# Sums of a linear-attention and GELU kernel in other TensorE tiles, and one more block of seven products

## The chip, the cores and the metric

The kernel runs on one core of a Trainium2 chip. Its time is the device time of the whole program in microseconds (us). The kernel before took 260.33 us as the median of three runs (260.18 to 260.61).

## The reference

First comes an attention without softmax. Queries and keys of 4 batches, 4 heads, 1088 tokens and 32 channels are each sketched twice (8 values each), and the outer product of the two sketches gives 64 features. Then

```
kv  = einsum('bhsf,bhsd->bhfd', k_p, v)
z   = sum(k_p, axis=2)
num = einsum('bhsf,bhfd->bhsd', q_p, kv)
den = einsum('bhsf,bhf->bhs', q_p, z)[..., None] + 1e-06
x   = (num / den), heads side by side: 4352 tokens x 128
out = gelu_exact(x @ w_in) @ w_out        # 128 -> 2048 -> 128
```

Everything is computed in float32. The two weight matrices arrive as 64-bit floats and are rounded to 32 bits on the chip.

## The kernel before, in words

The tokens are cut into eight chunks of 512, two for each batch (numbers 0 to 7), and one last chunk (8) with the 64 left-over tokens of each batch. The hidden width of 2048 is 16 pieces of 128, numbered by fi. The main loop (L1094) walks over a list `steps` of (chunk, fi); one entry is one step t. A step computes one hidden piece on TensorE (`hidden`, L686), ScalarE takes its GELU (L699), and a few steps later TensorE projects it back with `w_out`.

There are two ways to project. The plain way (`project`, L816) is one 128x128 matmul over 512 tokens for each fi. The other takes four pieces fi together as a block and does the two-by-two block multiplication with seven products instead of eight (`two_products`, L763). GpSimd forms the sums of tokens (`token_sums`, L733: four instructions, written to `bits_low`, `bits_a`, `bits_e`, `bits_m`) and once for each weight piece the sums of channels (`channel_sums`, L718: four instructions). TensorE then does seven pairs of 128x64 products over 256 tokens. The pairs are called fours, ones, sixes and twos after their names in the code; fours read `bits_low`, ones `bits_a`, sixes `bits_e`, twos `bits_m`. `drain` (L781) and `combine` (L806) put a chunk's results together. `USUAL = 8` says that chunks 0 and 1 take the first eight fi plainly. Their plain steps alternate, four by four: chunk 0 fi 0 to 3, chunk 1 fi 0 to 3, chunk 0 fi 4 to 7, chunk 1 fi 4 to 7; then chunk 0 fi 8 to 15, chunk 1 fi 8 to 15, and chunk 2 onward.

Among the steps stand pieces of the attention of later batches. They are entered by hand under a step number with `at(t, ...)` (L935), and within an engine the instructions stay in the order of the text (L1148 to L1154). For batches 1 to 3:

- `key_turn_blocks` (L356) and `features_of_all` (L939) sketch the keys: eight 64x32 matmuls. `outer_of_all` (L949) and `add_tokens` (L965) make the features and their sums over a partition's tokens, `k_s`, on VectorE. `turn_keys_rem` and `features_rem` (L985, L989) do the same for the left-over tokens with two 128x128 matmuls.
- `finish_keys` (L992) computes kv with `kv_sum` (L431): 36 matmuls of 128x32 tiles, 64 columns each, and z with `z_sum` (L440): four more. ScalarE copies kv out and `turn_kv` (L455) transposes it. `fold_z` (L446) writes z into the query sketch `S_abc`.
- `query_sketch` (L557) and `attend` (L605) are eight 64x32 matmuls each; `query_outer` (L574) between them is VectorE's. `turn_first_kv` (L499) does for batch 0, in four 128x32 matmuls, what `z_sum` does for the others.

PSUM has two banks for hidden pieces, two for projections, and two double banks (`work_banks`, L67) for the attention. `round_at` (L999) rounds a weight piece of 512 columns in two steps, with ScalarE and VectorE, for two pieces with a last product on GpSimd.

Of the kernel before, what the change touches and what calls it, by code (L numbers as in the profile page):

```python
# [8 lines left out]
FP = mybir.dt.float32  # L9
# [7 lines left out]
def kernel(  # L17
# [21 lines left out]
    F = R * R  # L39
# [13 lines left out]
    NMAIN = B * NCH  # L53
    NB = 4

    USUAL = 8
    NCHUNK = NMAIN + 1
    assert B == 4 and d_model == 128 == H * D == JC * D == 2 * F and H == 4 and REM == 64 and NCH == 2

# [7 lines left out]
    def work_banks():  # L67

        return wps.tile([128, 2, CW], FP, name="w_ps")
# [159 lines left out]

    kz_first = big.tile([128, 128], FP, name="kz_first")  # L230

    ones = big.tile([128, D], FP, name="ones")

    v_rem_aug = [big.tile([128, H, D if b else 2 * D], FP, name=f"v_rem_aug{b}") for b in range(B)]
    pool.memset(v_rem_aug[0], 0.0)
    pool.memset(v_rem_aug[0][:REM], 1.0)
    dve.memset(ones, 1.0)

    v_aug = [att.tile([128, NP, J, 2 * D], FP, name="sums") for r in range(2)]
    for t in v_aug:  # L240
# [185 lines left out]
    def kv_product(ps, lhsT, features, h, part, start=False, stop=False):  # L426

        pe.matmul(ps[h * D:(h + 1) * D, part * F:(part + 1) * F], lhsT=lhsT, rhs=features, start=start, stop=stop,  # L428
                  skip_group_check=True)
# [9 lines left out]

    def z_sum(b):  # L440

        ps = held["kv"][:, 0]
        for h in range(H):
            kv_product(ps, ones, k_s[b][:, h], h, 1, start=True, stop=True)

    def fold_z(b):  # L446
        sketch_of_z(b, held["kv"][:, 0], F)

    kv_T = {}

# [48 lines left out]
    def turn_first_kv():  # L499

        ps, zs = work_bank(), held["zs"]
        for h in range(H):
            c, r = h // 2, h % 2
            pe.matmul(ps[h * D:(h + 1) * D, :F], lhsT=zs[:, r], rhs=ident[:, c * F:(c + 1) * F], start=True, stop=True)
        sketch_of_z(0, ps, 0)


# [178 lines left out]
    def hidden(n, fi, by_halves=False):  # L686
        W = width[n]
        ps = first_banks.pop((n, fi)) if (n, fi) in first_banks else hidden_bank()
        w = w_tile(w_in_sb, fi)
        for rows in (slice(0, 64), slice(64, 128)) if by_halves else (slice(0, 128),):  # L690
            if (n, fi) not in begun:
                pe.matmul(ps[rows, :W], lhsT=w[:, rows], rhs=xT[n][:, :W], start=True, stop=True)  # L692
        if n < NCH and fi < USUAL:
# [5 lines left out]
        act.activation(out=g_of[n, fi][:, :W], in_=ps[:, :W], func=ACT.Gelu)  # L699
# [58 lines left out]
        return sums[n, b][j][:, e], T[j][:, k]  # L758

    def first_block(n):  # L760
        return USUAL // NB if n < NCH else 0

    def two_products(n, b, i):  # L763

        fours, ones_, sixes = [("4", "7", e, e) for e in range(2)], [("1", "5", e, e) for e in range(2)], ("6a", "6b", 0, 1)

        opens = b == first_block(n)
        order = fours + ([sixes] + ones_ if opens else ones_ + [sixes]) + [("2", "3", e, e) for e in range(2)]
        two = order[i]
        if opens and i == 0:  # L770
            acc[n] = [out_bank(), out_bank()]
        for name, e in zip(two[:2], two[2:]):
            half, bank, col = PLACE[name]
            moving, fixed = factor(n, b, name, e)

            pe.matmul(acc[n][bank][half * 64:(half + 1) * 64, col:col + HW], lhsT=fixed, rhs=moving,  # L776
                      start=opens and e == 0 and name in "4715", stop=b == NF // NB - 1, skip_group_check=True)
# [36 lines left out]
        return N[:, 1]  # L814

    def project(n, fi, parts=range(B // 2), cols=slice(None)):  # L816
        first, final = fi == 0, fi == (USUAL if n < NCH else NF) - 1
# [110 lines left out]
    w_out[0].fields()  # L928


    steps = [(n, fi) for f in range(0, USUAL, 4) for n in range(NCH) for fi in range(f, f + 4)]
    steps += [(n, fi) for n in range(NCHUNK) for fi in range(USUAL if n < NCH else 0, NF)]
    slots = {t: [] for t in range(len(steps) + LAG)}

    def at(t, f, *a):  # L935
        slots[t].append(lambda: f(*a))
# [52 lines left out]
    def features_rem(pair):  # L989
        key_features_rem(pair, held["rem"])  # L990

    def finish_keys(b, z=True):  # L992
        held["kv"] = work_banks()
        kv_sum(b, held["kv"][:, 0])
        if z:
            z_sum(b)
        take_kv(b, held["kv"][:, 0])

    def round_at(t, w, product_by=dve):  # L999
        r = []  # L1000
# [3 lines left out]
    for i, (t0, t1) in enumerate(((4, 6), (8, 10))):  # L1004
        round_at(t0, w_in_sb[i + 2])
        round_at(t1, w_out_sb[i + 2])
    round_at(12, w_in_sb[4], pool)
    at(13, channel_sums, 3)

    at(12, widen_v_rem, 1)  # L1010
    for r in range(2):
        at(14, key_turn_blocks, 1, r)
    round_at(14, w_out_sb[4], pool)
    at(15, query_turn, 2)
    at(16, features_of_all, 1)
    at(16, outer_of_all, 1)
    at(16, turn_keys_rem, 1)
    at(17, features_rem, 1)
    at(17, add_tokens, 1)
    at(18, channel_sums, 4)  # L1020

    at(21, finish_keys, 1, False)
    at(22, lambda: turn_kv(1, held["kv"]))
    at(23, z_sum, 1)
    at(23, fold_z, 1)
    at(23, query_turn, 3)
    at(24, query_sketch, 2)
    at(24, query_outer, 2)
    for i, t in enumerate((25, 26, 28)):
        at(t, channel_sums, i)  # L1030
    at(11, spread_sketches)
    at(40, repeat_first_z)
    for n in range(3, NCHUNK):

        t = (n - 1) * NF
        b = (n + 1) // 2
        keys = n % 2 and b < B
        if n > 3:
            at(t - 6, query_turn, n)
        if keys:  # L1040
            at(t - 1, sketch_and_attend, n)
            at(t - 1, features_of_all, b)
        else:
            at(t - 1, attend, n - 1)
            at(t - 1, query_sketch, n)
        at(t - 1, query_outer, n)
        if keys:
            for r in range(2):
                at(t - 3 if n > 3 else t - 4, key_turn_blocks, b, r)

        if n == NMAIN:
            at(t + 15, attend, n)
        if keys:
            at(t + 5 + (n == NCH + 1), outer_of_all, b)
            at(t + 5 + (n == NCH + 1), add_tokens, b)
            at(t + 8, widen_v_rem, b)
            at(t + 13, finish_keys, b)
            if b == 2:
                at(t + 13, turn_first_kv)
            at(t + 14, lambda b=b: turn_kv(b, held["kv"]))  # L1060
            at(t + 14, fold_z, b)


    products = {t: [] for t in range(len(steps) + LAG)}
    done = {t: [] for t in range(len(steps) + LAG + 1)}
    drains = {t: [] for t in range(len(steps) + LAG + 1)}
    for t, (n, fi) in enumerate(steps):
        if n < NCH and fi < USUAL:
            products[t + LAG].append((project, n, fi))
            if fi == USUAL - 1:  # L1070
                slots[t + LAG + 1 + 2 * n].append(lambda n=n: take_usual(n))
        elif n == NMAIN:
            at_ = max(t + LAG, (n * NF + 5) if fi < 3 else (n * NF + 6) if fi < 5 else 0)
            if fi < NF - 4:
                products[at_].append((project, n, fi))
            if fi == NF - 1:

                products[at_] += [(project, n, NF - f, (i,)) for f, i in ((4, 0), (3, 0), (2, 0), (4, 1), (1, 0), (3, 1),
                                                                          (2, 1), (1, 1))]
                done[at_ + 1].append(n)  # L1080
        elif fi % NB == NB - 1:
            b = fi // NB
            opens = b == first_block(n)
            late = int(n < NCH or n == NCH and opens)
            for later, pairs in ((3, 3), (4, 2), (5, 2)) if opens else ((2, 2), (3, 2), (4, 1), (5, 2)):
                later += late
                for i in range(pairs):
                    products[t + later].append((two_products, n, b, len([p for q in products.values() for p in q
                                                                        if p[:3] == (two_products, n, b)])))
            if b == NF // NB - 1:  # L1090
                drains[t + 6 + late].append(n)
                done[t + 12].append(n)

    for t in range(len(steps) + LAG):  # L1094
# [34 lines left out]
                f(*a)  # L1129
        if t < len(steps):  # L1130
            n, fi = steps[t]
            hidden(n, fi, by_halves=t >= 18 and (n < NMAIN or fi < 5))
# [52 lines left out]
```

## Time and profile before

| what | value |
|---|---|
| median of the runs | 260.33 us |
| the profiled execution: its own time | 260.86 us |
| the profiled execution: span from first to last instruction | 259.1 us |
| TensorE (PE) busy | 254.6 us, 98% |
| GpSimd (POOL) busy | 163.5 us, 63% |
| VectorE (DVE) busy | 151.6 us, 59% |
| ScalarE (ACT) busy | 114.9 us, 44% |

A float32 matmul leaves two records for each instruction in the trace, except the transposes by identity with one. "128*64" behind an operation is the part of the TensorE array that it uses, rows by columns; "128x512" is what it writes. Line numbers are those of the kernel before.

### The profile page before, as it was taken

What the parts mean: (1) busy time and instruction counts of PE and PEld (TensorE: products, weight loads), DVE (VectorE), ACT (ScalarE), POOL (GpSimd) and SP (SyncE); (2) the same over time, 40 slices, a digit from 0 to 9 for tenths busy, and PEclk for the clock granted to TensorE, in tenths of its full rate; (3) what the DMA queues carried; (4) which work ended last, traced back from release to release, by engine and by line L of the source; (5) the groups of instructions that cost most, each with busy time, mean ns of one, the idle gap of its engine ahead of it and who ended that gap; (6) DMA issues with size and microseconds to landing.
All of it is one profiled execution on the core that took longest, in us unless ns stands there. A gap on an engine that the chain in (4) does not pass through costs nothing.

```text
span 259.1 us, 5758 instructions
## 1 busy us (share of the span) xinstructions
PE 254.6 (98%) x2335; PEld 134.8 (52%) x2335; DVE 151.6 (59%) x313; ACT 114.9 (44%) x221; POOL 163.5 (63%) x173
## 2 busy tenths in 40 slices
PE   8999999999999999999999999999999999999994
PEld 7856444344444554444444454444445444445794
DVE  2886879969698997680178957630565043600330
ACT  4675767432625333533335334533353335334431
POOL 3404006799968776687758766867768776877200
PEclk9999999999999999999999999999999999999999
DMA  6469849820000101001000011020001100010020
GB/s 205 137 192 360 206 95 220 217 54 13 3 0 13 30 4 28 13 12 31 3 0 3 0 27 17 3 41 0 3 0 25 19 4 0 14 29 0 3 41 20
DMA packets 29530, 13.48 MB, mean 52 GB/s; under 512 B 21824, under 2 KB 27712, under 8 KB 29504
## 3 DMA queue, kind: packets, MB, share of 16 engines
q1 hardware_dynamic: 29472, 13.12, 20.8%
q8 instruction: 18, 0.29, 0.5%
q14 instruction: 8, 0.07, 0.1%
q10 hardware_dynamic: 32, 0.00, 0.0%
HBM read 10.88 MB, written 2.23 MB: 51 GB/s over the span
## 4 chain that ended last, share of the span: by engine, by line
PE 98%; ACT 0%; issue 0%; DVE 0%
PE h_ps L692 45%; PE o_ps L776 33%; PE o_ps L827 5%; PE w_ps L824 3%; PE w_ps L428 2%; PE w_ps L857 1%; PE w_ps L617 1%; PE w_ps L568 1%; PE o_ps L417 1%; PE w_ps L534 1%; PE h_ps L706 1%; PE h_ps L333 1%; PE w_ps L945 1%; PE w_ps L635 0%; PE w_ps L333 0%; PE h_ps L373 0%
## 5 line engine op out<-in xcount | busy, mean ns | idle before, releaser
L692 PE MATMUL h_ps<-xT,w_in 128*64 128x512 f32 (+3 forms) x514 | 137.1, 576 | 0.0
L699 ACT ACTIVATE block<-h_ps 128x512 f32<-128x512 f32 (+1 forms) x128 | 73.0, 571 | 120.2 <-PE h_ps L692 119.8
L776 PE MATMUL o_ps<-block,w_out 128*64 128x256 f32 x224 | 57.5, 379 | 0.0
L692 PEld LDWEIGHTS h_ps<-xT,w_in 128*64 128x64 f32 (+1 forms) x514 | 41.9, 142 | 29.2 <-issue 11.6
L741 POOL TENSOR_TENSOR bits_low<-block 128x512 f32<-128x512 f32 x28 | 35.6, 1273 | 27.6 <-ACT block L699 27.6
L776 PEld LDWEIGHTS o_ps<-block,w_out 128*64 128x64 f32 x224 | 30.5, 137 | 37.5 <-issue 26.7
L742 POOL TENSOR_TENSOR bits_a<-block 128x512 f32<-128x512 f32 x28 | 35.7, 1276 | 12.8 <-ACT block L699 12.8
L743 POOL TENSOR_TENSOR bits_e<-bits_a,block 128x512 f32<-128x512 f32 x28 | 36.1, 1290 | 2.2
L744 POOL TENSOR_TENSOR bits_m<-block,bits_e 128x512 f32<-128x512 f32 x28 | 35.8, 1280 | 2.2
L580 DVE STREAM_TRANSPOSE w_ps<-w_ps 128x512 f32<-128x512 f32 (+1 forms) x7 | 4.9, 693 | 42.8 <-PE w_ps L568 30.1
L776 PE MATMUL o_ps<-bits_low,small 128*64 128x256 f32 x112 | 29.0, 381 | 0.0
L776 PE MATMUL o_ps<-block,small 128*64 128x256 f32 x112 | 28.9, 381 | 0.0
L776 PE MATMUL o_ps<-bits_a,small 128*64 128x256 f32 x112 | 28.8, 379 | 0.0
L776 PE MATMUL o_ps<-bits_m,w_out 128*64 128x256 f32 x112 | 28.7, 379 | 0.0
L776 PEld LDWEIGHTS o_ps<-block,small 128*64 128x64 f32 x112 | 15.0, 137 | 17.6 <-issue 10.2
L791 DVE COPY sums<-o_ps 64x256 f32<-64x256 f32 x8 | 3.3, 416 | 34.4 <-PE o_ps L776 34.4
L776 PE MATMUL o_ps<-bits_e,small 128*64 128x256 f32 x112 | 17.1, 384 | 0.0
L827 PE MATMUL o_ps<-g,w_out 128*128 128x512 f32 (+1 forms) x34 | 16.5, 572 | 0.0
L776 PEld LDWEIGHTS o_ps<-bits_m,w_out 128*64 128x64 f32 x112 | 15.3, 137 | 0.0
L776 PEld LDWEIGHTS o_ps<-bits_a,small 128*64 128x64 f32 x112 | 15.2, 137 | 0.0
L776 PEld LDWEIGHTS o_ps<-bits_low,small 128*64 128x64 f32 x112 | 15.0, 137 | 0.0
L776 PEld LDWEIGHTS o_ps<-bits_e,small 128*64 128x64 f32 x112 | 7.5, 136 | 10.6 <-issue 9.1
(181 smaller groups left out, 303.2 us busy)
## 6 DMA issues: line engine op xcount, KB each, us to landing
out_dram<-oT SPq DMA_DIRECT2D x26, 64.0 KB, 2.2
block<-in_moe_w_in_dram SPq DMA_DIRECT2D x3, 512.0 KB, 7.2
block<-in_moe_w_out_dram SPq DMA_DIRECT2D x3, 512.0 KB, 11.6
k<-in_k_dram SPq DMA_DIRECT2D x12, 128.0 KB, 2.8
v<-in_v_dram SPq DMA_DIRECT2D x12, 128.0 KB, 3.4
q<-in_q_dram SPq DMA_DIRECT2D x24, 64.0 KB, 2.3
k<-in_k_dram SPq DMA_DIRECT2D x2, 256.0 KB, 2.8
q<-in_q_dram SPq DMA_DIRECT2D x2, 256.0 KB, 4.1
```

The costliest lines, as they stand in the source:

```text
L428: pe.matmul(ps[h * D:(h + 1) * D, part * F:(part + 1) * F], lhsT=lhsT, rhs=features, start=start, stop=stop, skip_group_check=True)
L580: dve.transpose(out=tok, in_=ps[:, :, :H2])
L692: pe.matmul(ps[rows, :W], lhsT=w[:, rows], rhs=xT[n][:, :W], start=True, stop=True)
L699: act.activation(out=g_of[n, fi][:, :W], in_=ps[:, :W], func=ACT.Gelu)
L741: pool.tensor_sub(out=s[3], in0=a11, in1=a21)
L742: pool.tensor_add(out=s[1], in0=a21, in1=a22)
L743: pool.tensor_sub(out=s[2], in0=s[1], in1=a11)
L744: pool.tensor_sub(out=s[4], in0=a12, in1=s[2])
L776: pe.matmul(acc[n][bank][half * 64:(half + 1) * 64, col:col + HW], lhsT=fixed, rhs=moving, start=opens and e == 0 and name in "4715", stop ...
L791: dve.tensor_copy(out=N[lo, 0, one], in_=a0[lo, one])
L824: pe.matmul(o_of[n][i][:, :128], lhsT=g[:, i * 128:(i + 1) * 128], rhs=w_tile(w_out_sb, fi), start=first, stop=final)
L827: pe.matmul(o_of[n][:, cols], lhsT=w_tile(w_out_sb, fi), rhs=g[:, cols], start=first, stop=final)
```

## The change

- `USUAL` becomes `[8, 4]`. Chunk 1 has fi 4 to 7 as a block of seven products. The order of steps is chunk 0 fi 0 to 3, chunk 1 fi 0 to 3, then chunk 0 fi 4 to 15, then chunk 1 fi 4 to 15. Chunk 0's plain projections of fi 4 to 7 are spread over steps 10, 12, 14 and 16. Its first block opens one step later than before, counted from its fi, and takes ones ahead of sixes.
- The rounding of `w_in[4]` goes ahead of `w_out[3]`; `w_out[4]` has its product on VectorE; `channel_sums` 2, 3, 4 are at steps 9, 14, 18, and 0, 1 at 25, 26. The keys of batch 1 go from steps 16 and 17 to 19 and 21.
- kv is computed inside the run of 64x32 matmuls: `kv_and_attend` puts it into an unused quarter of the double bank of `attend`, directly ahead of `attend` and `query_sketch`. For batch 1 there is no `attend` in that run.
- z is computed as four 128x64 matmuls (two accumulated in each half, with a left factor that has ones beside noughts) in a bank of its own, among the 128x64 matmuls of `hidden` and `two_products`. `turn_first_kv` becomes two 128x64 matmuls.
- `hidden` splits into halves from step 17, before from 18.

```diff
-    USUAL = 8
+    USUAL = [8, 4]
...
-    ones = big.tile([128, D], FP, name="ones")
+    ones = big.tile([128, 3, D], FP, name="ones")
...
-    dve.memset(ones, 1.0)
+    dve.memset(ones, 0.0)
+    dve.memset(ones[:, 1], 1.0)
...
     def z_sum(b):
-        ps = held["kv"][:, 0]
-        for h in range(H):
-            kv_product(ps, ones, k_s[b][:, h], h, 1, start=True, stop=True)
+        held["z"] = work_bank()
+        for r in range(2):
+            for c in range(NP):
+                pe.matmul(held["z"][c * F:(c + 1) * F, :F], lhsT=ones[:, 1 - r:3 - r].rearrange("p a d -> p (a d)"),
+                          rhs=k_s[b][:, 2 * c + r], start=r == 0, stop=r == 1)
...
     def turn_first_kv():
-        for h in range(H):
-            c, r = h // 2, h % 2
-            pe.matmul(ps[h * D:(h + 1) * D, :F], lhsT=zs[:, r], rhs=ident[:, c * F:(c + 1) * F], start=True, stop=True)
+        for c in range(NP):
+            pe.matmul(ps[c * F:(c + 1) * F, :F], lhsT=zs.rearrange("f r d -> f (r d)"), rhs=ident[:, c * F:(c + 1) * F],
+                      start=True, stop=True)
...
-    steps = [(n, fi) for f in range(0, USUAL, 4) for n in range(NCH) for fi in range(f, f + 4)]
-    steps += [(n, fi) for n in range(NCHUNK) for fi in range(USUAL if n < NCH else 0, NF)]
+    steps = [(n, fi) for n in range(NCH) for fi in range(4)]
+    steps += [(n, fi) for n in range(NCHUNK) for fi in range(4 if n < NCH else 0, NF)]
...
-    def finish_keys(b, z=True):
-        held["kv"] = work_banks()
-        kv_sum(b, held["kv"][:, 0])
-        if z:
-            z_sum(b)
-        take_kv(b, held["kv"][:, 0])
+    def kv_and_attend(b, n):
+        banks = held["kv"] = work_banks()
+        kv_sum(b, banks[:, 1, CW // 2:])
+        if n >= NCH:
+            attend(n, banks)
+        take_kv(b, banks[:, 1, CW // 2:])
...
-    round_at(12, w_in_sb[4], pool)
-    at(13, channel_sums, 3)
+    round_at(4, w_in_sb[2])
+    round_at(6, w_out_sb[2])
+    round_at(8, w_in_sb[3])
+    round_at(10, w_in_sb[4], pool)
+    round_at(12, w_out_sb[3])
+    at(6, spread_sketches)
+    at(9, channel_sums, 2)
     at(12, widen_v_rem, 1)
+    round_at(14, w_out_sb[4])
+    at(14, channel_sums, 3)
...
-    at(16, features_of_all, 1)
-    at(17, add_tokens, 1)
-    at(21, finish_keys, 1, False)
-    at(22, lambda: turn_kv(1, held["kv"]))
-    at(23, z_sum, 1)
-    at(24, query_sketch, 2)
+    at(19, features_of_all, 1)
+    at(21, features_rem, 1)
+    at(21, add_tokens, 1)
+    at(24, z_sum, 1)
+    at(26, kv_and_attend, 1, 1)
+    at(26, query_sketch, 2)
+    at(28, lambda: turn_kv(1, held["kv"]))
...
-            at(t - 1, attend, n - 1)
+            if n % 2 == 0 and b < B:
+                at(t - 1, kv_and_attend, b, n - 1)
+                at(t + 1, lambda b=b: turn_kv(b, held["kv"]))
+            else:
+                at(t - 1, attend, n - 1)
...
-            at(t + 13, finish_keys, b)
+            at(t + 13, z_sum, b)
+            at(t + 13, fold_z, b)
...
+            to = t + LAG + max(fi - NB, 0)
+            products[to].append((project, n, fi))
...
-            late = int(n < NCH or n == NCH and opens)
+            late = int(n < NCH or n == NCH and opens) + int(n == 0 and opens)
```

More of the change, by code (lines that the diff above doesn't have):

```diff
@@ L440, in z_sum @@
     def z_sum(b):
[L442 to L444 removed]
+        held["z"] = work_bank()
[3 more added lines that the diff above has]
+                          rhs=k_s[b][:, 2 * c + r], start=r == 0, stop=r == 1)
     def fold_z(b):
[L447 removed]
+        sketch_of_z(b, held["z"], 0)
     kv_T = {}
@@ L692, in hidden @@
                 pe.matmul(ps[rows, :W], lhsT=w[:, rows], rhs=xT[n][:, :W], start=True, stop=True)
-        if n < NCH and fi < USUAL:
+        if n < NCH and fi < USUAL[n]:
             g_of[n, fi] = mlp.tile([128, CW], FP, name="g", bufs=4)
@@ L760, in first_block @@
     def first_block(n):
-        return USUAL // NB if n < NCH else 0
+        return USUAL[n] // NB if n < NCH else 0
     def two_products(n, b, i):
@@ L767, in two_products @@
         opens = b == first_block(n)
-        order = fours + ([sixes] + ones_ if opens else ones_ + [sixes]) + [("2", "3", e, e) for e in range(2)]
+        order = fours + ([sixes] + ones_ if opens and n else ones_ + [sixes]) + [("2", "3", e, e) for e in range(2)]
         two = order[i]
@@ L816, in project @@
     def project(n, fi, parts=range(B // 2), cols=slice(None)):
-        first, final = fi == 0, fi == (USUAL if n < NCH else NF) - 1
+        first, final = fi == 0, fi == (USUAL[n] if n < NCH else NF) - 1
         if first:
@@ L1002, in round_at @@
         at(t + 1, lambda: (r[0].exponents(), r[0].mantissas(), r[0].signs(), r[0].product(product_by)))
-    for i, (t0, t1) in enumerate(((4, 6), (8, 10))):
-        round_at(t0, w_in_sb[i + 2])
-        round_at(t1, w_out_sb[i + 2])
-    round_at(12, w_in_sb[4], pool)
-    at(13, channel_sums, 3)
+    round_at(4, w_in_sb[2])
[5 more added lines that the diff above has]
+    at(9, channel_sums, 2)
     at(12, widen_v_rem, 1)
+    round_at(14, w_out_sb[4])
+    at(14, channel_sums, 3)
     for r in range(2):
         at(14, key_turn_blocks, 1, r)
-    round_at(14, w_out_sb[4], pool)
-    at(15, query_turn, 2)
-    at(16, features_of_all, 1)
-    at(16, outer_of_all, 1)
-    at(16, turn_keys_rem, 1)
-    at(17, features_rem, 1)
-    at(17, add_tokens, 1)
-    at(18, channel_sums, 4)
-    at(21, finish_keys, 1, False)
-    at(22, lambda: turn_kv(1, held["kv"]))
-    at(23, z_sum, 1)
-    at(23, fold_z, 1)
-    at(23, query_turn, 3)
-    at(24, query_sketch, 2)
-    at(24, query_outer, 2)
-    for i, t in enumerate((25, 26, 28)):
+    at(18, channel_sums, 4)
+    at(19, features_of_all, 1)
+    at(19, outer_of_all, 1)
+    at(19, turn_keys_rem, 1)
+    at(21, features_rem, 1)
+    at(21, add_tokens, 1)
+    at(21, query_turn, 2)
+    at(24, z_sum, 1)
+    at(24, fold_z, 1)
+    at(24, query_turn, 3)
+    at(26, kv_and_attend, 1, 1)
+    at(26, query_sketch, 2)
+    at(28, lambda: turn_kv(1, held["kv"]))
+    at(26, query_outer, 2)
+    for i, t in enumerate((25, 26)):
         at(t, channel_sums, i)
-    at(11, spread_sketches)
     at(40, repeat_first_z)
@@ L1035 @@
         t = (n - 1) * NF
-        b = (n + 1) // 2
+        b = (n + 1) // 2 if n % 2 else n // 2
         keys = n % 2 and b < B
@@ L1048 @@
             for r in range(2):
-                at(t - 3 if n > 3 else t - 4, key_turn_blocks, b, r)
+                at(t - 3 if n > 3 else 25, key_turn_blocks, b, r)
         if n == NMAIN:
@@ L1056 @@
             at(t + 8, widen_v_rem, b)
-            at(t + 13, finish_keys, b)
+            at(t + 13, z_sum, b)
+            at(t + 13, fold_z, b)
             if b == 2:
-                at(t + 13, turn_first_kv)
-            at(t + 14, lambda b=b: turn_kv(b, held["kv"]))
-            at(t + 14, fold_z, b)
+                at(t + 14, turn_first_kv)
     products = {t: [] for t in range(len(steps) + LAG)}
@@ L1067 @@
     for t, (n, fi) in enumerate(steps):
[L1068 to L1071, printed above, removed]
+        if n < NCH and fi < USUAL[n]:
+            to = t + LAG + max(fi - NB, 0)
+            products[to].append((project, n, fi))
+            if fi == USUAL[n] - 1:
+                slots[to + 1 + 2 * n].append(lambda n=n: take_usual(n))
         elif n == NMAIN:
@@ L1131 @@
             n, fi = steps[t]
-            hidden(n, fi, by_halves=t >= 18 and (n < NMAIN or fi < 5))
+            hidden(n, fi, by_halves=t >= 17 and (n < NMAIN or fi < 5))
         if t < len(steps) and steps[t][0] < NMAIN and steps[t][1] % NB == NB - 1:
```

## Prediction, made before the changed kernel ran

> **What bounds the kernel now.** I read the page's busy times first, then TensorE's waits, its instruction groups by shape, and the timeline of each engine around what the change touches.
>
> ```profile
> PE 254.6 (98%) x2335; PEld 134.8 (52%) x2335; DVE 151.6 (59%) x313; ACT 114.9 (44%) x221; POOL 163.5 (63%) x173
> ...
> PE w_ps L857 <- PEq L1169: 0.8, 1, 0.8
> PE h_ps L706 <- ACT xT L674: 0.2, 1, 0.2
> ```
>
> TensorE is busy for 98% of the span, and its list of waits has only these two entries, both before 16 us. So the end is set by how long TensorE's own stream is. A removed matmul counts in full, as long as no other engine then comes too late.
>
> The price of each piece is the distance between starts in TensorE's timeline:
>
> ```profile
> 93.31 1.03 PE L692 MATMUL h_ps<-xT,w_in 128*64 128x512 f32 x4
> 94.26 1.10 PE L428 MATMUL w_ps<-k_p,v 128*32 128x64 f32 x64
> 95.18 0.29 PE L428 MATMUL w_ps<-k_p_rem,v_rem_aug 128*32 128x64 f32 x8
> 95.29 0.29 PE L428 MATMUL w_ps<-k_s,ones 128*32 128x64 f32 x8
> 95.40 0.29 PE L504 MATMUL w_ps<-ident,z_cols 128*32 128x64 f32 x8
> 95.63 0.43 PE L776 MATMUL o_ps<-block,small 128*64 128x256 f32 x1
> ...
> 95.89 0.38 PE L776 MATMUL o_ps<-block,small 128*64 128x256 f32 x1
> ...
> 98.48 1.03 PE L692 MATMUL h_ps<-xT,w_in 128*64 128x512 f32 x4
> 99.44 0.66 PE L617 MATMUL w_ps<-q_pT,kz 64*32 64x256 f32 x16
> 99.90 0.64 PE L568 MATMUL w_ps<-qT,S_abc 64*32 64x256 f32 x16
> 100.47 0.65 PE L776 MATMUL o_ps<-bits_e,small 128*64 128x256 f32 x4
> 100.95 1.03 PE L692 MATMUL h_ps<-xT,w_in 128*64 128x512 f32 x4
> ```
>
> A hidden piece or a plain projection takes 0.86 us (27.48, 28.34, 29.20 in a plain stretch). A pair of block products has starts 0.215 us apart inside it and takes 0.43. A change of tile shape costs extra: the hidden piece at 93.31 should give way at 94.17, and kv starts at 94.26 (0.10 to enter). The four z_cols matmuls need 0.11, so the products should start at 95.51; they start at 95.63, and their first half-pair takes 0.26 instead of 0.215 (0.17 to leave). Leaving the 64x32 run costs 0.20 by the same reading.
>
> **The Trainium skill.** "TensorEngine Tiling (Array Packing)", Key Properties, says that changing the tiling mode, not just the tile, drains TensorE. The trace agrees: 0.10 to 0.20 us at each change. It also means that kv (128x32) beside `attend` (64x32) is still a change of mode. "TensorE: Matmul & The Clock Gate", LDWEIGHTS, says that a weight load goes by its columns; z in 64-column tiles loads twice the columns. At 10.16 us 32 matmuls of 128x64 tiles with 33 columns take 1.00 us, 0.06 a pair, so loads do not bind there. "GPSIMD Engine Reference", Specifications, says that GpSimd shares its SBUF interfaces with VectorE and contends with some of its instructions. The trace fits: four channel sums of 128x128 take 2.94 us at 42.09 and 1.82 at 46.36.
>
> **The change, part by part, on TensorE** (negative is saved)
>
> 1. Chunk 1 fi 4 to 7: four projections (4 x 0.86 = 3.43) become seven pairs (7 x 0.43 = 3.01): -0.43.
> 2. Batch 1: kv stood alone, from 51.12 (hidden at 49.40 plus 1.72) to 52.46 (next hidden at 52.41, itself 0.05 longer): 1.34. The sketch alone, from 56.95 to 57.70, took 0.75. Joined: enter 0.10, kv 9 groups of four at 0.115 = 1.035, change inside the run, sketch 0.43, leave 0.20. No row shows 128x32 to 64x32 directly; it is bounded by 0 and by the 0.22 of a full way out, and I take the 0.10 of a way in. Sum 1.87 against 2.09: -0.22 (-0.32 to -0.10).
> 3. Batch 1, z: from 54.40 to 54.81 = 0.40. Now two pairs of 64 columns among 128x64 tiles, 4 x 0.054 = 0.22: -0.19. If loads bound them it could be 0.35.
> 4. Batch 2: 94.17 to 95.67 = 1.50 becomes kv 1.035, change 0.10, z 0.22, z_cols 0.11: -0.04 (-0.14 to +0.08). Batch 3: 1.40 becomes 1.355: -0.05 (same width).
> 5. The left-over keys of batch 1 move from plain 128x128 surroundings (steps 16, 17) among the halves (19, 21). The transpose then has a change after it (0.14, as at 46.53 to 47.53, where 0.86 took 1.00), and L399 has one on both sides: 0.35 against 0.17. Together +0.32.
> 6. Pure hidden steps must wait for the bank of two steps ago. Before, step 20 came at 49.40 instead of 49.25. After, the same 0.15 is lost at step 19, since step 17's GELU ends near 44.0. Net 0.
>
> Sum: -0.61. The tail after chunk 3 has the same instructions.
>
> **What the moves may uncover.** Chunk 0 now runs through, so steps 10 to 19 hold four projections where there were eight; step 20 comes at about 46.0 (49.4 before), while VectorE and GpSimd have the same rounding to do. I followed each queue with the durations of its rows.
>
> - Weights: `w_in[3]` is ready at 34.6 as before, and is now needed at 35.2, not 42.9. It was never closer; covering it are 0.6 us, and GpSimd's four channel sums of piece 2 now run beside it. If that slows VectorE as it did at 42.3 (0.67 for 0.42, 0.94 for 0.69) up to 0.3 us remains. `w_in[4]`: ScalarE and VectorE end at 37.3, GpSimd's product (1.29) at 38.7, needed at 40.4. The GpSimd copy of `v_rem`, which waited for its DMA until 37.71, now stands behind this product and holds nobody; the SP queue's loads keep their order.
> - Work that only changes its engine or place: `w_out[4]`'s product goes from GpSimd (1.26) to VectorE (0.69), ready near 45.2 and next wanted by channel sums 4 at 48.8. The second `memset` of `ones` falls into VectorE's wait of 2.5 us for the sketches' DMA. Without these covers they would cost their own length on their queue.
> - GpSimd: `w_out[3]` is rounded after `w_in[4]`, ready at 40.7 (38.1 before). Then channel sums 3 take 2.94 (as at 42.09) to 43.7, the sums of chunk 0's first block 5.18 (49.34 to 54.52) to 48.8, channel sums 4 1.82 to 50.7, the first sum of the second block 1.28 to 51.9. TensorE reaches that block's fours at step 22: 46.0, hidden 0.86, three pairs 1.29, hidden 0.86, L399 0.35, two pairs 0.86, hidden 0.86, two pairs 0.86 = 51.9. A tie; before, this had some 5 us of room (ready 55.8, used 61.1).
> - VectorE: features of batch 1. The L399 at 49.1 gives `a_rem`, which ScalarE takes behind step 21's GELU at 49.7; then VectorE's product 0.33, reductions 4.11, `k_s` 0.87: ready at 55.25. TensorE reaches z at step 24, after its hidden piece: 55.3. A tie too (before: ready 54.04, used 54.50).
> - Later queues have room: `drain(0)`'s read of the second bank ends near 59.5, fours of chunk 1 start at 61; the query of chunk 2 is ready near 67.5, needed at 69. At batch 2 kv's bank is free of `fold_z` near 98.1, needed near 98.9.
>
> Two ties with some tenths of spread each cost about 0.2 us (a delay at the first gives room to the second). -0.61 + 0.2 = -0.4. On the profiled span that is 258.7; the profiled execution lies 0.5 above the median of the runs, so I put the same -0.4 on the median: 259.9 us.
>
> ```profile
> 42.09 0.65 POOL L728 TENSOR_TENSOR small<-w_out 128x128 f32<-128x128 f32 x1
> ...
> 46.36 0.45 POOL L728 TENSOR_TENSOR small<-w_out 128x128 f32<-128x128 f32 x1
> ...
> 49.34 1.28 POOL L741 TENSOR_TENSOR bits_low<-block 128x512 f32<-128x512 f32 x1 [1.16 <-ACT block L699]
> ...
> 54.52 1.27 POOL L741 TENSOR_TENSOR bits_low<-block 128x512 f32<-128x512 f32 x1
> ...
> 49.07 4.07 DVE L969 TENSOR_REDUCE w_ps<-k_p 128x128 f32<-128x1024 f32 x2
> ```
>
> The reader sees the same four-fold sum at two prices, and GpSimd going from one block to the next without a gap: it is the queue that can be late.
>
> **Rivals**
>
> - *GpSimd sets the pace between 44 and 58 us (slower).* If the channel sums both take 2.94 and the token sums 1.61 instead of 1.27 (as L743 does once, at 79.74), the second block's first sum comes at 40.7 + 2.94 + 6.6 + 2.94 + 1.6 = 54.8, 2.9 us late; time 262.6. It decides from a lateness of 1.1 us on: 0.61 are then eaten and 0.5 lost. For it: the tie and VectorE's rounding beside. Against: at 46.36 and 49.34 VectorE ran long multiplies and reductions, and those are what it runs here too. Middle of this case 261.4.
> - *No waits, and the change inside a run is free:* -0.61 - 0.3 = -0.9; time 259.4.
> - *The merge is worth nothing:* 0.22 for each change inside a run (three times +0.12) and loads that bind z (three times +0.13) turn -0.61 into +0.14, and with the 0.2 of waits +0.34: time 260.7, which is no change that can be told. For it: no row of before has either. Against: a way in costs 0.10, and the 33-column pairs above run at 0.06.
>
> **How the numbers follow.** Chances: my sum with small waits 0.50 (259.7 to 260.2), no waits 0.22, GpSimd or VectorE late 0.20, merge worth nothing 0.08. About 0.2% (0.52 us, 259.81) is what a measurement of this kernel can tell from no change. About a third of the first case and all of the second lie beyond it: 0.18 + 0.22, faster 0.40. Slower than 260.85: most of the third, 0.18. The rest 0.42. The range leaves out the lowest part of the second case and the upper part of the third: 259.3 to 261.0.
>
> **What would show it.** Right: TensorE's groups lose four 128x512 projections and gain seven pairs of 128x256 products; kv at about 58.5 and 99 directly ahead of L620/L571 rows; no wait of TensorE above 0.3 us at steps 22 and 24. Wrong: an entry in TensorE's waits on GpSimd's `bits_low` or on `k_s`, hidden pieces at 35.2 waiting on `w_in`, or a gap over 0.15 between kv and the 64x32 matmuls behind it.

## The result and the profile after

The changed kernel takes 262.07 us (median of 6 runs, 261.73 to 262.56), the kernel before beside it 260.56 us (6 runs, 260.18 to 261.15). The ratio is 1.0059 with a 95% interval of 1.0043 to 1.0076: 1.5 us slower, where 0.4 us faster was forecast. The profiled execution took 262.56 us, its span is 260.8 us.

Starts of different executions differ by up to a microsecond before the main loop (the first matmul on `w_in` comes between 14.64 and 15.63 us in the traces used here, whatever the kernel). So traces are compared below by one distance: from that first matmul to the end of the span. It is 243.86 us before and 245.16 after, +1.30. Line numbers from here on are those of the changed kernel; most lie three higher than before.

The busy row of the page, which answers to the one shown of before:

```profile
PE 255.2 (98%) x2353; PEld 137.0 (53%) x2353; DVE 154.1 (59%) x315; ACT 114.5 (44%) x221; POOL 169.4 (65%) x176
```

TensorE still shows 98%, and this row alone would hide the loss. The three longest entries of TensorE's list of waits (microseconds in total, number, longest) show it; two more, of 0.2 us, lie ahead of the main loop.

```profile
PE w_ps L860 <- PEq L1178: 0.8, 1, 0.8
PE w_ps L429 <- PE h_ps L695: 0.6, 1, 0.6
PE o_ps L779 <- POOL bits_low L744: 0.4, 1, 0.4
```

Two of these three are new. The third line is the wait for GpSimd's `bits_low` that the prediction named as a sign of being wrong. The second is kv of batch 2. The reader should not stop at the 0.4: TensorE's timeline (start, duration) around the third line shows what it cost.

```profile
52.16 0.38 PE L779 MATMUL o_ps<-block,w_out 128*64 128x256 f32 x1
52.17 0.38 PE L779 MATMUL o_ps<-bits_m,w_out 128*64 128x256 f32 x1
52.38 0.59 PE L779 MATMUL o_ps<-block,small 128*64 128x256 f32 x2
53.39 0.43 PE L779 MATMUL o_ps<-bits_low,small 128*64 128x256 f32 x1 [0.42 <-POOL bits_low L744]
...
53.88 0.59 PE L695 MATMUL h_ps<-xT,w_in 128*64 128x512 f32 x1
54.09 0.38 PE L779 MATMUL o_ps<-bits_low,small 128*64 128x256 f32 x1
54.31 1.02 PE L695 MATMUL h_ps<-xT,w_in 128*64 128x512 f32 x3
```

A pair of products is two matmuls, one in each column half of the array. They normally start together (52.16 and 52.17). At 52.38 the half that reads `block` goes ahead with two matmuls; the other half waits for `bits_low` until 53.39, 1.0 us, of which the list books 0.42, since the first half was busy for the rest. Afterwards one half stays ahead: the hidden piece of step 23 starts at 53.88 in one half and at 54.31 in the other. Without the wait it would have started at 52.38 + 4 x 0.215 = 53.24, so its earlier half is 0.64 us late and its later half 1.07.

GpSimd's timeline says why `bits_low` came at 53.33 and not at 51.9 (with this run's start, which is 0.41 us later than that of the kernel before, 52.3):

```profile
37.83 1.39 POOL L298 TENSOR_TENSOR w_in<-bits_m,bits_e 128x512 f32<-128x512 f32 x1 [3.20 <-DVE bits_e L293]
...
41.80 0.57 POOL L731 TENSOR_TENSOR small<-w_out 128x128 f32<-128x128 f32 x1 [1.35 <-DVE w_out L298]
...
43.88 1.72 POOL L744 TENSOR_TENSOR bits_low<-block 128x512 f32<-128x512 f32 x1
45.57 1.71 POOL L745 TENSOR_TENSOR bits_a<-block 128x512 f32<-128x512 f32 x1
47.36 1.61 POOL L746 TENSOR_TENSOR bits_e<-bits_a,block 128x512 f32<-128x512 f32 x1
49.04 1.27 POOL L747 TENSOR_TENSOR bits_m<-block,bits_e 128x512 f32<-128x512 f32 x1
50.28 0.46 POOL L731 TENSOR_TENSOR small<-w_out 128x128 f32<-128x128 f32 x1
...
52.06 1.27 POOL L744 TENSOR_TENSOR bits_low<-block 128x512 f32<-128x512 f32 x1
```

GpSimd starts on the channel sums when `w_out[3]` is rounded, and from 41.80 on it has no gap. Three of the four token sums of the first block take 1.6 to 1.7 us; the same lines take 1.27 elsewhere. VectorE's timeline over the same time:

```profile
38.00 1.50 DVE L274 TENSOR_SCALAR bits_a<-block 128x512 uint32<-128x512 uint32 x1
...
41.02 0.69 DVE L298 TENSOR_TENSOR w_out<-bits_m,bits_e 128x512 f32<-128x512 f32 x1
...
44.39 1.76 DVE L293 SCALAR_TENSOR_TENSOR bits_e<-block,bits_r 128x512 uint32<-128x512 uint32 x1
46.19 1.64 DVE L298 TENSOR_TENSOR w_out<-bits_m,bits_e 128x512 f32<-128x512 f32 x1
```

The first line is a mask of the rounding of `w_out[3]`. It runs beside GpSimd's product of `w_in[4]` and takes 1.50 us, where the same line takes 0.42 in quiet, and the piece is ready at 41.71. The last two lines belong to the rounding of `w_out[4]`; they take 1.76 and 1.64 us for operations of 0.69. It looks as if VectorE and GpSimd hold each other up, which e9b below tests.

The second wait is in batch 2. VectorE's timeline there, with the chunk's `combine` (L813 to L841) ahead of `fold_z` (L486 to L489):

```profile
93.72 0.43 DVE L978 TENSOR_TENSOR k_s<-w_ps,k_p_rem 64x256 f32<-64x256 f32 x1
...
94.82 1.21 DVE L813 TENSOR_TENSOR sums<-sums 64x256 f32<-64x256 f32 x1
96.04 1.41 DVE L814 TENSOR_TENSOR sums<-sums 64x256 f32<-64x256 f32 x1
...
98.21 0.71 DVE L841 STREAM_TRANSPOSE oT<-sums 128x512 f32<-128x512 f32 x1
98.95 0.23 DVE L486 TENSOR_TENSOR z_s<-w_ps,sT 128x64 f32<-128x64 f32 x1
...
99.55 0.17 DVE L489 TENSOR_TENSOR S_abc<-w_ps,own_r 128x16 f32<-128x16 f32 x1
```

The same stretch in the kernel before (its line numbers):

```profile
92.62 0.43 DVE L975 TENSOR_TENSOR k_s<-w_ps,k_p_rem 64x256 f32<-64x256 f32 x1
...
98.47 0.17 DVE L486 TENSOR_TENSOR S_abc<-w_ps,own_r 128x16 f32<-128x16 f32 x1
```

And TensorE's timeline of the stretch in the changed kernel:

```profile
94.39 1.03 PE L695 MATMUL h_ps<-xT,w_in 128*64 128x512 f32 x4
95.25 0.40 PE L446 MATMUL w_ps<-k_s,ones 128*64 128x64 f32 x8
...
97.21 0.28 PE L506 MATMUL w_ps<-ident,z_cols 128*64 128x64 f32 x4
98.19 1.03 PE L695 MATMUL h_ps<-xT,w_in 128*64 128x512 f32 x4
99.82 1.10 PE L429 MATMUL w_ps<-k_p,v 128*32 128x64 f32 x64 [0.61 <-PE h_ps L695]
```

kv writes the bank that z used, and that bank is free when `fold_z` has read it, at 99.72. The hidden piece at 98.19 gave way at 99.05, a way into another tile shape would have put kv at 99.15. The list names the hidden piece as releaser, but that was done; by the times it is VectorE, and e3 below tests it.

### The profile page after: what moved, and what is told of

Same layout as the page of the kernel before. It is cut to its first block, busy times and chain, and to the rows that moved or that the text cites. A ratio compares the mean times of both kernels' runs of the same rounds, so it can differ in the third digit from the quotient of the medians.

```text
span 260.8 us, 5802 instructions
## 1 busy us (share of the span) xinstructions
PE 255.2 (98%) x2353; PEld 137.0 (53%) x2353; DVE 154.1 (59%) x315; ACT 114.5 (44%) x221; POOL 169.4 (65%) x176
## 4 chain that ended last, share of the span: by engine, by line
PE 91%; POOL 4%; DVE 2%; issue 1%; ACT 0%; DVEq 0%
PE h_ps L695 41%; PE o_ps L779 33%; PE o_ps L830 3%; PE w_ps L827 3%; PE w_ps L860 1%; PE w_ps L620 1%; PE w_ps L571 1%; PE w_ps L429 1%; POOL bits_low L744 1%; PE w_ps L537 1%; PE o_ps L418 1%; PE h_ps L709 1%; PE h_ps L334 1%; POOL bits_a L745 1%; POOL bits_e L746 1%
## 5 line engine op out<-in xcount | busy, mean ns | idle before, releaser
L702 ACT ACTIVATE block<-h_ps 128x512 f32<-128x512 f32 (+1 forms) x132 | 75.4, 572 | 121.3 <-PE h_ps L695 119.3
L779 PE MATMUL o_ps<-block,w_out 128*64 128x256 f32 x232 | 59.8, 379 | 0.0
L744 POOL TENSOR_TENSOR bits_low<-block 128x512 f32<-128x512 f32 x29 | 37.4, 1288 | 27.9 <-ACT block L702 27.9
L745 POOL TENSOR_TENSOR bits_a<-block 128x512 f32<-128x512 f32 x29 | 37.5, 1292 | 12.1 <-ACT block L702 12.1
L746 POOL TENSOR_TENSOR bits_e<-bits_a,block 128x512 f32<-128x512 f32 x29 | 37.7, 1301 | 2.3
L747 POOL TENSOR_TENSOR bits_m<-block,bits_e 128x512 f32<-128x512 f32 x29 | 37.1, 1279 | 2.3
L779 PE MATMUL o_ps<-bits_a,small 128*64 128x256 f32 x116 | 30.0, 380 | 0.0
L779 PE MATMUL o_ps<-block,small 128*64 128x256 f32 x116 | 30.0, 379 | 0.0
L779 PE MATMUL o_ps<-bits_m,w_out 128*64 128x256 f32 x116 | 29.8, 379 | 0.0
L830 PE MATMUL o_ps<-g,w_out 128*128 128x512 f32 (+1 forms) x26 | 12.4, 563 | 0.0
```

The lines of the kernel that those rows point to most:

```text
L744: pool.tensor_sub(out=s[3], in0=a11, in1=a21)
L745: pool.tensor_add(out=s[1], in0=a21, in1=a22)
L746: pool.tensor_sub(out=s[2], in0=s[1], in1=a11)
L747: pool.tensor_sub(out=s[4], in0=a12, in1=s[2])
```

## The experiments

The theory after the comparison: the stream of TensorE did become shorter, and two waits of the change's own making ate it: about 1.0 us for GpSimd's first sum of chunk 0's last block, 0.65 for kv's bank. The rivals: the joined runs or the seven products are themselves dearer than worked out; or GpSimd only looks late. All times below are ratios to the kernel before, run on the same chip in the same minutes (not all the rows on one chip); a difference of ratios is turned to microseconds with 260.7.

| run | ratio to before (95%) | first `w_in` matmul to end |
|---|---|---|
| changed kernel | 1.0059 (1.0043 to 1.0076) | 245.16 |
| e1_sums_alone | 1.0058 (1.0045 to 1.0071) | 245.37 |
| e2_blocks_alone | 1.0073 (1.0061 to 1.0086) | 245.68 |
| e3_combine_later | 1.0027 (1.0017 to 1.0037) | 244.50 |
| e5_wait_moved | 1.0018 (1.0011 to 1.0025) | 244.38 |
| e6_both_waits | 0.9994 (0.9987 to 1.0002) | 243.66 |
| e4_sums_later_alone | 1.0070 (1.0056 to 1.0085) | 245.69 |
| e9_less_rounding | 1.0074 (1.0060 to 1.0089) | 245.70 |
| e9b_less_rounding_free | 1.0014 (1.0007 to 1.0021) | 244.17 |
| e7_left_over_early | 0.9990 (0.9981 to 0.9999) | 243.67 |
| e10_product_by_vectore | 0.9976 (0.9967 to 0.9984) | 243.48 |
| e1b_sums_free | 0.9997 (0.9987 to 1.0007) | 243.65 |

**One part at a time.** e1 is the kernel before with only the part on kv and z: `z_sum`, `turn_first_kv` and `kv_and_attend` as in the changed kernel, and for batch 1

```diff
-    at(21, finish_keys, 1, False)
-    at(22, lambda: turn_kv(1, held["kv"]))
     at(23, z_sum, 1)
...
+    at(24, kv_and_attend, 1, 1)
     at(24, query_sketch, 2)
+    at(26, lambda: turn_kv(1, held["kv"]))
```

> The kernel before with only the sums changed: kv inside the runs of 64x32 matmuls, z and the first batch's z in 128x64 tiles. USUAL stays 8 and the steps stay in their old order. Theory (two waits ate a gain of some 0.6 us; one of them is kv of batch 2 waiting 0.6 us for its bank, which fold_z frees late behind combine(1)): that wait is here too, since it has nothing to do with the blocks; the sums save 0.5 and the wait takes 0.6, so +0.1 us against before (-0.2 to +0.4), with TensorE idle some 0.5 us before kv near 98 us. Rival (the new sums are dear by themselves, by their changes of tile shape): +0.8 us or more without a wait. Rival (the sums are harmless and all the loss comes from the blocks): -0.5 us.

e2 is the changed kernel with `z_sum`, `turn_first_kv` and `finish_keys` as before, and for batch 1

```diff
+    at(23, finish_keys, 1, False)
+    at(24, lambda: turn_kv(1, held["kv"]))
     at(24, z_sum, 1)
...
-    at(26, kv_and_attend, 1, 1)
...
-    at(28, lambda: turn_kv(1, held["kv"]))
```

> The changed kernel with kv and z as before (kv alone at step 23, z at 24, batches 2 and 3 as before): only the seven products for fi 4 to 7 of chunk 1, the run through chunk 0 and the moved rounding and keys. Theory: saves 0.43 in products, pays 0.3 for the left-over keys among half tiles and 1.0 to 1.2 for the wait on GpSimd's first sum of the second block near 52 us: +0.9 us against before (+0.6 to +1.3); no wait near 98 us. Rival (the loss is in the sums): -0.1 us.

Both expectations failed: each part alone is as slow as the whole. But each alone had a wait of my own placing. The longest entries of TensorE's list of waits in e1:

```profile
PE w_ps L446 <- DVE k_s L978: 0.8, 1, 0.8
PE w_ps L860 <- PEq L1176: 0.8, 1, 0.8
PE w_ps L429 <- PE h_ps L695: 0.6, 1, 0.6
```

A line of TensorE's timeline in e2 (start, duration, and in brackets the idle time before it; the line number is that of the kernel before):

```profile
58.70 0.32 PE L428 MATMUL w_ps<-k_s,ones 128*32 128x64 f32 x8 [0.72 <-ACT kz L459]
```

In e1, kv no longer stands ahead of z, and TensorE is at z before `k_s` is; in e2, `turn_kv` and z share a step and a bank, and z waits for ScalarE's copy. What can be read from them is that the wait for kv's bank (0.6) belongs to the part on kv and z, and the wait for `bits_low` (0.5 in e2) to the part on blocks. For the worth of the parts they say nothing; e1b below does.

**Each wait alone.** e3 puts chunk 1's `combine` and store three steps later, behind `fold_z` in VectorE's queue:

```diff
-                done[t + 12].append(n)
+                done[t + (15 if n == 1 else 12)].append(n)
```

e5 puts the last block of chunk 0 one step later, and z behind it:

```diff
-    at(24, z_sum, 1)
-    at(24, fold_z, 1)
-    at(24, query_turn, 3)
+    at(25, z_sum, 1)
+    at(25, fold_z, 1)
+    at(25, query_turn, 3)
...
-            for later, pairs in ((3, 3), (4, 2), (5, 2)) if opens else ((2, 2), (3, 2), (4, 1), (5, 2)):
+            for later, pairs in ((3, 3), (4, 2), (5, 2)) if opens else ((3, 2), (4, 3), (5, 2)) if n == 0 else ((2, 2), (3, 2), (4, 1), (5, 2)):
```

> The changed kernel with combine and store of chunk 1 three steps later, so that VectorE does fold_z of batch 2 ahead of them and frees the bank early. Nothing else. Theory: the wait of 0.6 us before kv of batch 2 goes away, -0.6 us against the changed kernel (-0.4 to -0.7), +0.9 against before. Rival (kv waits there for something else, or the next wait takes its place at the drain of chunk 2): within 0.2 us of the changed kernel.

> The changed kernel with the second block of chunk 0 asking for its sums later: no pair at step 22, fours at 23, ones and sixes at 24, twos at 25; and z of batch 1 at step 25 instead of 24. TensorE's work is the same, instruction by instruction. Theory (GpSimd's sum is 1.0 us late for step 22, and VectorE's k_s would be next at step 24): -1.1 us against the changed kernel (-0.8 to -1.3), +0.4 against before. Rival (TensorE's stream itself is longer there, waits are not the cause): within 0.2 us of the changed kernel.

Measured: e3 is 0.0032 under the changed kernel, 0.8 us, 0.66 in the traces (by the times a little more than expected); e5 0.0041, 1.1 us, 0.78 in the traces. In each the wait aimed at is gone from TensorE's list and the other is still there. In e3's timeline of VectorE `fold_z` of batch 2 ends at 96.23, ahead of `combine`:

```profile
96.06 0.17 DVE L489 TENSOR_TENSOR S_abc<-w_ps,own_r 128x16 f32<-128x16 f32 x1
...
97.99 1.43 DVE L813 TENSOR_TENSOR sums<-sums 64x256 f32<-64x256 f32 x1
```

And in e3's timeline of TensorE kv follows its hidden piece without a wait, 0.96 after it:

```profile
97.95 1.03 PE L695 MATMUL h_ps<-xT,w_in 128*64 128x512 f32 x4
98.91 1.10 PE L429 MATMUL w_ps<-k_p,v 128*32 128x64 f32 x64
```

**Both.** e6 is e3 and e5 at once.

> The changed kernel with both edits at once: chunk 0's last block of products one step later with z behind it (step 25), and chunk 1's combine three steps later. Theory (the change's loss is two waits of TensorE of its own making, 1.1 us for GpSimd's first sum and 0.65 us for kv's bank, on a stream that became shorter): the two gains add up, -1.7 us against the changed kernel, which puts it 0.1 to 0.3 us under the kernel before (ratio 0.9995 to 0.999), and TensorE's list of waits has no entry after 30 us. Rival (the stream itself did not become shorter by the 0.61 us worked out, because the block products, or the joined runs, cost more than their sum): the waits go but the time stays 0.3 us or more above the kernel before.

Measured: 0.9994 (0.9987 to 1.0002), 1.7 us under the changed kernel as the theory had it, and level with the kernel before within what can be measured. TensorE's whole list of waits:

```profile
PE w_ps L860 <- PEq L1178: 0.8, 1, 0.8
```

The distances nearly add up: -0.66 and -0.78 alone make -1.44, and both edits together give -1.50, from 245.16 to 243.66. What is left is 0.20 under the kernel before, not 0.61. Of the difference, 0.14 is still GpSimd's: the hidden piece of step 23 starts at 52.15, so TensorE is at the fours at 53.01, and the half that reads `bits_low` starts at 53.15. The rest lies in the sum of the stream itself, taken apart below.

**What stands behind the first wait.** e4 is e5 without the move of z.

> The changed kernel with only the last block of chunk 0 a step later; z stays at step 24. Theory (k_s, ready at about 56.4 us, is VectorE's own lateness, hidden behind the wait for GpSimd): TensorE now reaches z at about 55.1 us and waits 1.2 us for k_s instead, so the time stays within 0.4 us of the changed kernel. Rival (k_s only looks late because TensorE was late; VectorE would have it ready): the time falls by 1.1 us as in the run where z moved too.

Measured: 1.0070, level with the changed kernel (1.0059) within the intervals. TensorE's timeline has the second tie of the prediction, `k_s`, in the place of the first wait:

```profile
56.26 0.45 PE L446 MATMUL w_ps<-k_s,ones 128*64 128x64 f32 x8 [1.17 <-DVE k_s L978]
```

So VectorE really is late as well, and in the changed kernel this lateness (`k_s` ready at 56.42, z at 56.48) lay hidden behind GpSimd's.

**Why GpSimd is late.** e9 takes away the last steps of the rounding of `w_out[4]` on VectorE.

```diff
-    round_at(14, w_out_sb[4])
+    plain = []
+    at(14, lambda: (plain.append(Rounding(w_out_sb[4])), plain[0].low_words(), plain[0].mantissa_fields()))
+    at(15, lambda: (plain[0].mantissas(), act.copy(out=w_out_sb[4], in_=plain[0].m)))
```

> The changed kernel, but the fifth piece of w_out gets no exponent, sign and product: ScalarE copies its mantissas instead, so this part of the computation is left out. VectorE loses one operation of 0.42, one of 1.76 and one of 1.64 us that run beside GpSimd's sums of the first block. Theory (GpSimd is late because VectorE's rounding and GpSimd's sums slow each other): the sums of that block take about 1.27 each, 5.1 us together and not 6.4, the first sum of the last block is ready at about 52.0 us, TensorE does not wait for it, and the time falls by about 1.1 us. Rival (GpSimd's sums take 1.7 us there for another reason, such as reading beside ScalarE's GELU): they keep their 6.4 us, the wait stays 1.0 us, the time falls by less than 0.2 us.

The total did not fall (1.0074), so the expectation failed on the time. The wait for `bits_low` was gone, but ScalarE's copy, which waits for VectorE's mantissas, stood ahead of GELU steps, and TensorE's timeline has a hidden piece waiting 1.44 us for its bank at 44.60. That was the experiment's own doing. From the sketch of batch 1's keys on (L948, behind that wait) to the end it is 214.37 us against 215.42 in the changed kernel, 1.05 shorter. e9b settles it, with the copy two steps later:

```diff
-    at(15, lambda: (plain[0].mantissas(), act.copy(out=w_out_sb[4], in_=plain[0].m)))
+    at(15, lambda: plain[0].mantissas())
+    at(17, lambda: act.copy(out=w_out_sb[4], in_=plain[0].m))
```

> The run with less rounding once more, with ScalarE's copy of the mantissas behind three GELU steps and not ahead of them (there it kept a hidden piece's bank 1.4 us and ate the gain). The sign, exponent and product of the fifth piece of w_out are left out again. Theory (VectorE's rounding and GpSimd's sums slow each other): no wait of TensorE for GpSimd's first sum, and 1.0 to 1.1 us less than the changed kernel in the times, so ratio about 1.002 to the kernel before; the wait of 0.6 us for kv's bank stays. Rival (the gain after 45 us in the earlier run came only from TensorE being 1.4 us later): TensorE again waits over 0.5 us for the first sum, and less than 0.5 us is gained.

Measured: 1.0014, 1.2 us under the changed kernel, 0.99 in the traces, and no wait for `bits_low`. GpSimd's timeline in e9b:

```profile
43.95 1.28 POOL L744 TENSOR_TENSOR bits_low<-block 128x512 f32<-128x512 f32 x1
45.19 1.27 POOL L745 TENSOR_TENSOR bits_a<-block 128x512 f32<-128x512 f32 x1
...
50.90 1.27 POOL L744 TENSOR_TENSOR bits_low<-block 128x512 f32<-128x512 f32 x1
```

They start at nearly the same time as in the changed kernel (43.88) and take 1.28 (L746 too) where those took 1.72, 1.71 and 1.61. The next block's first sum starts 0.99 us earlier, counted from the first `w_in` matmul (35.44 and 36.43). So the hold of the two engines on each other is shown to be the cause. It also made `k_s` late: counted from the first `w_in` matmul, `k_s` is ready at 39.82 in e9b and at 40.79 in the changed kernel, so that the 0.99 us covers both. The 1.49 us of L274 beside GpSimd's earlier product is still there in e9b; e10 below takes that away.

**The part on kv and z, without those waits.** e1b is e1 with z at step 24, kv and the sketch at 25, what follows on them moved along, and e3's edit.

> The kernel before with only the part on kv and z (kv in the sketch's and the numerators' runs, z and the first z in 128x64 tiles), placed so that none of the waits of the first such run arises: z at step 24, kv with the sketch at 25, chunk 1's combine three steps later. By the prediction's steps 2 to 4 the stream is 0.50 us shorter; the pure hidden steps 18 to 22, which kv no longer parts, wait 0.3 us more for their banks. Theory (the steps' sums are right): 0.1 to 0.3 us less than the kernel before, ratio 0.999 to 0.9996. Rival (joined runs and narrow z cost more than worked out): 0.2 us or more above the kernel before.

Measured: 0.9997 (0.9987 to 1.0007), 0.21 less than before in the traces. The ratio can't be told from either no change or the gain expected; it does exclude the rival's 0.2 us or more above. In the traces e1b and e6 end alike (243.65, 243.66), but the difference is not the price of the part on blocks. In e1b six hidden pieces follow each other without products between them and wait for their banks: from 47.38 to 52.90 they take 0.36 us more than 6 x 0.86. In the kernel before that loss is 0.15, in e6 about 0.10. Without it the part on kv and z would be worth some 0.42 us, and the part on blocks would cost some 0.2 in e6, with the 0.14 that GpSimd still takes. These two are estimates from the traces; no run shows them.

**A kernel faster than both.** e7 is e6 with the left-over keys back among plain matmuls:

```diff
-    at(19, turn_keys_rem, 1)
-    at(21, features_rem, 1)
+    at(14, turn_keys_rem, 1)
+    at(16, features_rem, 1)
```

e10 is e7 with the product of `w_in[4]` on VectorE:

```diff
-    round_at(10, w_in_sb[4], pool)
+    round_at(10, w_in_sb[4])
```

> As the run with both edits, and the left-over keys of batch 1 go back among plain 128x128 matmuls (transpose at step 14, their features at step 16, before the halves begin). Theory (among the halves they cost 0.32 us of changes of tile shape, step 5 of the prediction): 0.3 us less than the run with both edits, about 0.5 us under the kernel before (ratio 0.998). Rival (the changes of shape are hidden, or the time comes back as a wait for a hidden piece's bank): no difference from the run with both edits, within 0.15 us.

> As the run with both edits and early left-over keys, and the product of w_in's fifth piece on VectorE (0.69) instead of GpSimd (1.39, beside which VectorE's next mask takes 1.64 instead of 0.42 us). Theory (TensorE's pace up to 54 us is set by GpSimd's first sum of the last block, which hangs on VectorE's rounding of the fourth piece of w_out): that piece is ready 0.4 us earlier, so is the first sum, the 0.47 us that the early keys gained until step 22 is kept now, and the time is 0.4 us less than in that run: 0.6 us under the kernel before, ratio 0.9975 to 0.998. Rival (TensorE's own stream, or the halves running out of step, sets the pace): no difference from that run, within 0.15 us.

e7 measured 0.9990: no difference from e6 that can be told, as its rival had it. The traces show where the gain went, and it isn't the rival's bank. Counted from the first `w_in` matmul, the hidden piece of step 23 comes at 36.31 in e7 and at 36.78 in e6, 0.47 earlier. At step 25 they are level again (40.88 and 40.85): TensorE stands at the last block's fours, at GpSimd's first sum. With e10 that sum is 0.4 us sooner relative to it, since VectorE is no longer held. VectorE's timeline in e7:

```profile
37.34 1.64 DVE L274 TENSOR_SCALAR bits_a<-block 128x512 uint32<-128x512 uint32 x1
```

The same place in e10's:

```profile
37.63 0.69 DVE L298 TENSOR_TENSOR w_in<-bits_m,bits_e 128x512 f32<-128x512 f32 x1
...
38.58 0.51 DVE L274 TENSOR_SCALAR bits_a<-block 128x512 uint32<-128x512 uint32 x1
```

VectorE takes on a product of 0.69 and still ends sooner, because the mask behind it takes 0.51 and not 1.64. e10 measured 0.9976 (0.9967 to 0.9984): 260.05 us against 260.75 on the same chip, faster than both kernels. By the runs it is 0.36 us under e7, as expected, though the two intervals overlap a little; the traces show 0.19, because that execution of e10 lost 0.2 us at `x_tok` ahead of the loop (its hidden pieces are already 0.2 late at step 17). GpSimd still sets the pace in it: its sum is ready at 52.85 and TensorE is there at 52.65 (hidden at 51.79 plus 0.86).

## Why the prediction was wrong

The method, summing TensorE's stream and then asking which wait comes up, found the right places. Two sizes in the second half were wrong.

- **"GpSimd: ... the first sum of the second block 1.28 to 51.9", a tie.** This is the step that failed most. TensorE was there when forecast (52.38, or 51.97 with this run's later start taken off), but the sum was 1.0 us late. Three terms were off. "The sums of chunk 0's first block 5.18" took 6.40, 1.22 more. "`w_out[3]` ... ready at 40.7" came at 41.3 on the same clock (41.71 in the trace), 0.6 more; GpSimd's product of `w_in[4]` ran beside VectorE's mask of that piece, which took 1.50 instead of 0.42. The channel sums, put at 2.94, took 2.08, which by luck hid 0.86 of this. e9b prices the slow token sums at 0.99 us in the traces, and e10 gains 0.4 us at this place from the mask. The argument "at 46.36 and 49.34 VectorE ran long multiplies and reductions, and those are what it runs here too" was the error: what VectorE ran beside the token sums was `w_out[4]`'s rounding, whose product the change moves from GpSimd to VectorE, and which the prediction had on its own list, with the cost of that product covered. The Trainium skill, "SBUF — State Buffer", SBUF: two separate sides, says that VectorE and GpSimd share a port pair as an exclusive lock: of a VectorE operation with two SBUF inputs and a GpSimd operation that reads SBUF, the one that starts first keeps the pair for its whole length. The trace agrees: with two SBUF inputs L293 and L298 took 1.76 and 1.64 for 0.69, and GpSimd 1.7 for 1.28; multiplies on a PSUM operand (L963, 2.35 for two) left GpSimd's 1.27 as it was. The prediction had the sharing and the pair of prices (2.94 and 1.82) in hand and put the dear price on the wrong four instructions.
- **"At batch 2 kv's bank is free of `fold_z` near 98.1, needed near 98.9."** Counted as room of 0.8; it was a wait of 0.6, priced at 0.66 by e3. The term that failed is the need, 98.9: that fits the start of the 64x32 matmuls before (99.44) less the half microsecond gained until then. But the change itself takes kv (1.1 us) and its transposes out of steps 45 and 46. From the hidden piece of step 45 to that of step 47 TensorE needed 5.17 us before (93.31 to 98.48) and needs 3.80 now (94.39 to 98.19). It is there 1.37 sooner, and 0.8 - 1.37 gives the wait of 0.6. VectorE's queue does not come sooner with it: from the end of `k_s` to the end of `fold_z` it took 5.59 us before (93.05 to 98.64) and takes 5.57 now (94.15 to 99.72). No case of the prediction had this wait. Work moved later must be priced against the new clock of every engine, not against the old one of TensorE.
- **"Features of batch 1 ... ready at 55.25 ... a tie too."** Right in its place and late by 0.75 (56.42, or 56.0 with this run's start taken off). The lateness comes from the same rounding: `a_rem` was there at 50.17, but VectorE took it up (L405) only at 51.23, behind the multiplies of L963 that had queued behind L298; in e9b, which leaves L293 and L298 out, it takes it up as soon as it is there and `k_s` is 0.97 sooner. Behind the first wait it cost nothing; e4 shows that it costs 1.2 us as soon as that wait is moved alone. "A delay at the first gives room to the second" was right.
- **The sum of the stream, -0.61.** +1.30 in the traces, less 0.99 for GpSimd and 0.66 for the bank, leaves -0.35; e6 gives -0.34 by another way, its -0.20 less the 0.14 of GpSimd. Terms that can be read: the change from kv to the 64x32 matmuls, taken at 0.10 without any row, is right: kv starts at 60.22 and the sketch at 61.37, 1.15 for 1.035 and 0.115. z at 0.22 is right (the hidden piece gives way to z at 95.25, products follow at 95.48), and so are the two `z_cols` matmuls (0.11).
- **The left-over keys, step 5, "+0.32".** Too small: e7 saves 0.47 until step 23. L400 among the halves takes 0.10 in and 0.36 to the next start, and the pair behind it 0.27 instead of 0.215. With 0.15 more for this term the sum is -0.46, against the -0.35 read. The 0.1 left isn't explained by a run.
- **The rivals.** "GpSimd sets the pace" is what happened, at its lower end: a lateness of 1.0, where it was to decide from 1.1 on. It had the slow token sums right (6.6; they took 6.4) and the channel sums wrong (twice 2.94; they took 2.1 and 1.8). Its chance was 0.20, and its own arithmetic (261.4 in the middle) is 0.7 short; the second wait, which it lacked, makes up that much. "The merge is worth nothing" is out by the 1.15 and 0.23 above. "No waits" is out.

What remains of the change's idea is small: e6, without both waits, is 0.2 us under the kernel before in the traces and not to be told from it in the times. Of these runs only e10, where the left-over keys go back and GpSimd's queue comes sooner too, is clearly faster than the kernel before.

## What to carry to other kernels

When an engine near its limit is given less to do, follow the helpers' queues with the durations of what will run beside them, not with those of a quiet stretch: here elementwise operations of VectorE on two SBUF inputs and GpSimd's sums each waited for the other (0.69 became 1.76, 1.28 became 1.72), so moving work between these two can cost more than its length or, as in e10, give some back. A buffer that was free in time may not be once work ahead of its reader's consumer has moved away, because the reading engine's queue does not move with it. And an experiment that moves one part alone makes new neighbours: its own waits have to be read before its time is.

## What the runs showed that I had not expected

- The two column halves of TensorE do not wait for each other. When one half waits for an operand, the other goes on with its next matmul, and they stay out of step over the following steps (53.88 and 54.31 in the changed kernel, 38.23 and 38.53 from the first `w_in` matmul in e10). The list of waits books only the part in which both stand: 0.42 of 1.0 us.
- A mask of integers with a single SBUF input (L274, 0.42 alone) is held by GpSimd as well, which two SBUF inputs do not explain. It takes 1.64 us in e7 and 1.50 in the changed kernel. In e7 GpSimd's product runs from 37.17 for 1.39 us, to 38.56, and L274 ends 0.42 later; in the changed kernel it ends 0.28 after the product (39.22 and 39.50).
- `combine`'s additions L813 and L814 took 1.21 and 1.41 us in the changed kernel (1.23 and 1.41 before), beside GpSimd's sums, while L814 took 0.42 in e3. That is probably the same hold, inside the queue that made kv wait; no run takes it apart.
